# A fused attention and MLP-mixer kernel: the order, PSUM banks and gates of every queue read from a table instead of a list scheduler, and one fp32r matmul woven with two bf16 ones

## The chip, the cores and the metric

The kernel runs on one core of one Trainium2 chip. The metric is the device time of one execution, in microseconds (us); lower is better. Before the change three runs took 354.62, 355.6 and 358.28 us, so the median is 355.6 us.

## The reference

Eight batches of a linear attention with eight heads, then a mixer block on its output; everything is given and returned in fp32.

```python
kv  = einsum('bhsd,bhse->bhde', k, v)            # B=8, H=8, S=576, D=64
out = einsum('bhsd,bhde->bhse', q, kv)
out = out / sqrt(mean(out*out, -1) + 1e-6) * g_norm
x   = out.transpose(0,2,1,3).reshape(8, 576, 512)
a1  = alpha1*x + beta1
u   = x + lam * einsum('ts,bsd->btd', w_tok, a1)     # token mixing, 576 x 576
a2  = alpha2*u + beta2
y   = u + lam * (relu(a2 @ w_ch1) @ w_ch2)           # channel mixing, 512 -> 2048 -> 512
```

## The kernel before

The program is written in two steps. First the body of the kernel records operations ("ops") with what they read and write; each op gets an index in the order in which it is recorded (0 to 1415), and belongs to one queue: PE (TensorE), ACT, DVE, POOL or SP. A PE op holds several matmuls (`mm`, line 120); the others hold one instruction or one DMA. `_add` (line 75) derives the dependencies. Then `schedule` (line 135) orders everything, `synchronize` (line 387) works out the semaphore waits that this order needs, and `emit` (line 447) writes the instructions. Each engine executes its queue strictly in the order that comes out.

`schedule` is a list scheduler. It plays the program on a clock of its own: every op has a cost guessed from its size, due times are propagated backwards from the main stream of matmuls, a table `P.shift` (line 1283) moves single ops, and a table `P.gate` (line 1298) adds dependencies ("op 9 after op 31"). PE has two streams. The main one (`ch1`, `ch1_tail`, `ch2`) goes in its recorded order; the fill stream (all else) is put between where it is ready, with a margin of 0.3 us. PSUM has eight banks of 128x512 fp32; main ops take banks 0 to 3 in turn, fill ops banks 4 to 7.

Where a ready fill op of fp32r matmuls meets a ready main op of bf16 matmuls, the two become one unit and are woven (line 428): one fp32r matmul, one bf16 matmul, and so on. While the main stream has not begun, an fp32r or fp32 op is woven with throw-away matmuls on the tile `fil` instead (`idler`, line 379; L597 in the profile), which keep TensorE busy.

What the work is, by the names that the prediction uses:

- Start. SP loads q, k and v of batch 0 in pairs of heads (`load_pair`, L611, 288 KB each), four pairs of q of batch 1, and the token weights (`wl`, L629, 1152 KB; `wlt`, L631, 144 KB). `qt_early` (L698 on POOL, L703 on PE) transposes q, `kv_first` (L725) makes k'v, `norm_half` (L864) multiplies by q and normalises (L807 to L833). `wt_group` (L1081, L1084) transposes the token weights; ACT copies them to bf16 (L1087); `wsums` (L1103, L1110, L1113, L1118) adds rows of sums. `tok_half` (L929) is the token mixing of batch 0, its result is added to x on DVE (L937), `a2_pair` (L968, L972) transposes that into the layout for the channel mixing.
- Steady state, for each batch: `kv` (L749, L755, then L766 on ACT and L768 on DVE) and `norm` (L843, then Square on ACT L807, DVE L810, ACT L813, DVE L816 to L825), all fp32r matmuls of 128 columns; `tok` (L914, bf16, five matmuls of 512 columns, added on DVE L921); `a2_dma` (two POOL instructions, L986 and L989, and a transposing DMA from SP, L993); `ch1` (L1002, four matmuls of 512 columns, relu on ACT L997) sixteen times, `ch2` (L1031, four units of four matmuls for each of four blocks of tokens), `finish` (DVE L1058, POOL or DVE L1063, a store from SP, L1066). The last 64 tokens of two batches go together (`tok_tail` L948, `ch1_tail` L1014).
- Weights of the channel mixing come in five transfers issued by POOL (`load_w1` L1163, `load_w2` L1169) between its other work, in the same POOL queue as the loads of k and v (`load_kv`, L1186, L1190).
- End. The last block of tokens of the last batch is cut into 256, 128 and 128 columns (L1042), each with its own `finish` and two small stores (L1070).

The weave before is these lines:

```python
    def woven(f, m):                      # line 428: f fp32r, m bf16
        out, i, j = [], 0, 0
        n, k = len(f.fns), len(m.fns)
        while i < n or j < k:
            if i < n and (j >= k or i * k <= j * n):
                out.append((f, i)); i += 1
            else:
                out.append((m, j)); j += 1
```

Of the kernel before, what the change touches and what calls it, by code (L numbers as in the profile page):

```python
# [11 lines left out]
ACT = mybir.ActivationFunctionType  # L12
# [11 lines left out]

class Op:


    __slots__ = ("bias", "q", "kind", "cost", "lat", "fns", "pri", "idx", "deps", "raw", "alloc",
                 "tiles", "start", "end", "pos", "waits", "inc", "clock", "slot", "nbytes",
                 "val", "margin", "tag", "narrow", "urgent", "ns")  # L30

    def __init__(self, q, kind, cost, lat, fns, pri, idx):
        self.q, self.kind, self.cost, self.lat = q, kind, cost, lat
        self.fns, self.pri, self.idx = fns, pri, idx
        self.deps, self.raw = set(), set()
        self.alloc, self.tiles = [], []
        self.start = self.end = self.pos = None
        self.waits, self.inc, self.clock = [], False, None
        self.slot = self.nbytes = self.val = self.ns = None
        self.margin = 0.0  # L40
        self.tag, self.narrow, self.urgent = "", False, False
# [12 lines left out]
class Prog:  # L54
    ENGINES = ("PE", "ACT", "DVE", "POOL")

    def __init__(self, nc, stack):
# [7 lines left out]
        self.main, self.fill = [], []  # L65
        self.bias = 0.0
        self.reach = 24
        self.warm, self.began, self.early, self.lead = 6.0, False, 45.0, 100.0
        self.t0, self.pace, self.last, self.shift = 31.0, 1.28, None, {}
        self.gate = {}  # L70
# [4 lines left out]
    def _add(self, o, r, w, after):  # L75
# [10 lines left out]
        for key in w:  # L86
# [21 lines left out]
    def op(self, q, cost, fn, r=(), w=(), pri=0.0, lat=0.15, after=()):  # L108
        o = Op(q, "c", cost, lat, [fn], self.bias + pri, len(self.ops))
        o.bias = self.bias  # L110
        return self._add(o, r, w, after)

    def dma(self, q, slot, nbytes, fn, r=(), w=(), pri=0.0, after=(), issue=0.55):
        o = Op(q, "d", issue, 0.0, [fn], self.bias + pri, len(self.ops))
        o.slot = slot
        o.nbytes, o.ns = nbytes if isinstance(nbytes, tuple) else (nbytes, 20.0)
        o.bias = self.bias
        return self._add(o, r, w, after)

    def mm(self, stream, cols, fns, r=(), w=(), slow=False, after=(), margin=0.3,  # L120
           urgent=False):

        n = len(fns)
        per = cols * MM_NS + 0.0025
        each = slow if isinstance(slow, float) else {"r": 0.213}.get(slow, 0.109)
        o = Op("PE", "w" if slow and each is not slow else "m",
               n * (max(per, each) if slow else max(per, 0.056)),
               0.24, fns, self.bias, len(self.ops))
        o.bias = self.bias
        o.margin, o.narrow, o.urgent = 0.0 if urgent else margin, cols < 512, urgent  # L130
        (self.main if stream == "main" else self.fill).append(o)
        return self._add(o, r, w, after)


    def schedule(self):
        for i, j in self.gate.items():
            self.ops[i].deps.add(self.ops[j])
        due, t = {}, self.t0
        for o in self.main:
            due[o] = t  # L140
            t += o.cost * self.pace
        after = {}
        for o in self.ops:
            for y in o.deps:
                after.setdefault(y, []).append(o)
        order, left = [], {o: len(after.get(o, ())) for o in self.ops}
        stack = [o for o in self.ops if not left[o]]
        while stack:
            o = stack.pop()
            order.append(o)  # L150
            for y in o.deps:
                left[y] -= 1
                if not left[y]:
                    stack.append(y)
        for o in order:
            d = due.get(o, 1e6)
            for y in after.get(o, ()):
                if y in due:
                    d = min(d, due[y] - o.cost - o.lat - (2.5 if o.kind == "d" else 0.0))
            if d < 1e6:  # L160
                due[o] = d
        for o in self.ops:
            if o.kind == "d":
                o.pri += self.shift.get(o.idx, 0.0)
            elif o in due and o.pri - o.bias > -900:
                o.pri = due[o] + self.shift.get(o.idx, 0.0)
            elif o.pri - o.bias > -900:
                o.pri = 1e4 + o.pri
        self.fill.sort(key=lambda o: o.pri)
        queues = {e: [] for e in ("ACT", "DVE", "POOL", "SP")}  # L170
        for o in self.ops:
            if o.q != "PE":
                queues[o.q].append(o)
        for q in queues.values():
            q.sort(key=lambda o: (o.pri, o.idx))
        main, fill = list(self.main), list(self.fill)
        self.main0 = set(self.main)
        free = {e: 0.7 for e in list(queues) + ["PE"]}
        owner = [None] * 8
        rings = {e: deque() for e in ("SP", "POOL", "ACT")}  # L180
        t, left = 0.0, len(self.ops)
        events = {0.7}
        self.sequence = []
        self.idle = []
        last_fill = False
        INF = 1e9

        def ready_at(o):
            m = 0.0
            for y in o.deps:  # L190
                if y.end is None:
                    return INF
                m = max(m, y.end - y.lat if y.q == o.q == "PE" else y.end)
            return m

        def bank_at(b):
            x = owner[b]
            if x is None:
                return -1.0
            m = 0.0  # L200
            for y in x.ops:
                if y.end is None:
                    return INF
                m = max(m, y.end)
            return m

        def place(o, t):
            got = []
            for tile in o.alloc:
                c = [(bank_at(b), b) for b in self.pools[tile.pool] if b not in got]  # L210
                c = [x for x in c if x[0] <= t + 1e-9]
                if not c:
                    return None
                got.append(min(c)[1])
            return got

        def can(o, t, margin=0.0):
            return ready_at(o) + margin <= t + 1e-9 and place(o, t) is not None

        def take(o, t, cost=None):  # L220
            nonlocal left
            for tile, b in zip(o.alloc, place(o, t)):
                tile.bank = b
                if owner[b] is not None:
                    o.deps.update(owner[b].ops)
                owner[b] = tile
            o.start = t
            if o.kind == "d":
                rings[o.q].append([o, t + (1.9 if o.q == "POOL" else 1.1), o.nbytes, False, o.ns,
                                   o.slot[0] == "t"])  # L230
            else:
                o.end = t + (o.cost if cost is None else cost) + o.lat
                events.add(o.end)
            if o.margin:
                events.add(o.end + 0.3)
            left -= 1

        def begin(a):
            for r in rings.values():
                if r and r[0][1] <= a + 1e-9:  # L240
                    r[0][3] = True

        def heads():
            return [r[0] for r in rings.values() if r and r[0][3]]

        def soonest(h):
            whole = sum(x[4] for x in h)
            return min(x[2] * whole / x[4] for x in h)

        def flow(a, z):  # L250

            while True:
                if not heads():
                    begin(a)
                h = heads()
                n = min([a + soonest(h) if h else min([r[0][1] for r in rings.values() if r] + [z]),
                         z])
                whole = sum(x[4] for x in h)
                for x in h:
                    x[2] -= (n - a) * x[4] / whole  # L260
                done = [x for x in h if x[2] <= 1e-6]
                for r in rings.values():
                    if r and r[0][3] and r[0][2] <= 1e-6:
                        r.popleft()
                a = n
                if done:
                    begin(a)
                for x in done:
                    o = x[0]
                    if x[5]:  # L270
                        rings[o.q].appendleft([o, a + 0.6, 0.05, False, 20.0, False])
                    else:
                        o.end = a + (0.1 if o.slot[0] == "t" else 2.0 if len(h) > 1 else 1.2)
# [1060 lines left out]
```

## Time and profile before

| What | Value |
|---|---|
| Runs | 354.62, 355.6, 358.28 us (median 355.6) |
| Profiled execution, span from its first to its last instruction | 354.8 us |
| Instructions | 5512 |
| TensorE matmul busy | 341.3 us (96%), 2208 matmuls |
| VectorE (DVE) busy | 189.8 us (54%) |
| ScalarE (ACT) busy | 149.0 us (42%) |
| GpSimd (POOL) busy | 161.4 us (45%) |
| Moved by DMA | 48.76 MB, mean 137 GB/s |

The profiled execution's own time is its span, 354.8 us; it lies 0.8 us under the median of the runs shown. A line of the profile names the source line, engine and operation, then what is written and read ("ps<-w,hh" writes PSUM from two tiles). Matmuls are pipelined: the record of one lasts longer than the time until the next can start, so a matmul's price is read from the distance of starts. PEclk is the granted TensorE clock, 1 or 9 being full speed.

### The profile page before, as it was taken

The numbers are of one execution on the slowest core, as the hardware profiler recorded it, in microseconds if no ns is written. First come the engines' busy times: TensorE is split into PE (matmuls) and PEld (weight loads), VectorE is DVE, ScalarE is ACT, GpSimd is POOL, SyncE is SP. The second block draws the span as 40 slices with busy tenths as digits, with TensorE's granted clock in tenths as the row PEclk, the third lists the DMA queues.
The fourth block names the chain that finished last, engine by engine and source line by source line (L and its number), as shares of the span: only waits on it lengthen the run. The fifth ranks groups of instructions, "written<-read, shape, count | busy, mean of one in ns | idle before, by whom it ended". The sixth has DMA issues, their size and how long they took to land.

```text
span 354.8 us, 5512 instructions
## 1 busy us (share of the span) xinstructions
PE 341.3 (96%) x2208; PEld 198.4 (56%) x2241; DVE 189.8 (54%) x343; ACT 149.0 (42%) x291; POOL 161.4 (45%) x151
## 2 busy tenths in 40 slices
PE   4979999999999999999999999999999999999994
PEld 3858964454664664466556545564476444444644
DVE  3475778204685579636745676459444963210043
ACT  3335397004940386126823366136552273026400
POOL 2397410965308940985058612973192306930000
PEclk9989999999999999999999999999999999999999
DMA  7999899969598399138963995239922110330012
GB/s 241 267 336 161 139 251 230 144 110 198 120 262 134 90 232 213 31 93 195 247 61 76 221 173 124 46 116 258 175 33 89 59 31 15 75 105 0 2 69 79
DMA packets 107952, 48.76 MB, mean 137 GB/s; under 512 B 81997, under 2 KB 99925, under 8 KB 107928
## 3 DMA queue, kind: packets, MB, share of 16 engines
q1 hardware_dynamic: 82312, 27.71, 42.9%
q0 software_dynamic: 25616, 20.71, 34.0%
q8 instruction: 17, 0.28, 0.3%
q14 instruction: 7, 0.06, 0.1%
HBM read 38.82 MB, written 9.44 MB: 136 GB/s over the span
## 4 chain that ended last, share of the span: by engine, by line
PE 87%; DMA 5%; SPq 2%; POOL 2%; DVE 1%; issue 1%; ACT 0%; DVEq 0%; POOLq 0%
PE ps L1031 31%; PE ps L1002 31%; PE ps L914 8%; PE ps L1014 4%; PE ps L843 3%; DMA hh<-in_moe_w_tok_dram 2%; PE ps L749 2%; DMA w<-in_k_dram 2%; PE ps L597 1%; SPq L611 1%; PE ps L929 1%; POOL a1f L986 1%; PE ps L948 1%; PE ps L1081 1%; PE ps L1042 1%; DMA lam_bc<-in_moe_lam_dram 1%
## 5 line engine op out<-in xcount | busy, mean ns | idle before, releaser
L1031 PE MATMUL ps<-w,hh 128*128 128x512 bf16 x543 | 135.3, 383 | 0.7 <-issue 0.3
L1002 PE MATMUL ps<-a2m,w 128*128 128x512 bf16 x501 | 117.8, 381 | 1.0 <-DVE tmp L1058 0.4
L997 ACT ACTIVATE hh<-ps 128x512 bf16<-128x512 f32 x144 | 84.8, 597 | 64.3 <-PE ps L1002 54.9
L1031 PEld LDWEIGHTS ps<-w,hh 128*128 128x128 bf16 x560 | 52.9, 97 | 58.8 <-issue 1.6
L1002 PEld LDWEIGHTS ps<-a2m,w 128*128 128x128 bf16 x512 | 48.7, 98 | 56.5 <-DVE tmp L1058 1.3
L986 POOL TENSOR_TENSOR a1f<-xm,a_bc 128x512 f32<-128x512 f32 x28 | 35.5, 1273 | 68.6 <-DVE xm L921 68.3
L1058 DVE TENSOR_TENSOR tmp<-ps,lam_bc 128x512 f32<-128x512 f32 (+2 forms) x38 | 25.1, 661 | 69.8 <-PE ps L1031 56.5
L1063 POOL TENSOR_TENSOR xm<-xm,tmp 128x512 f32<-128x512 f32 x28 | 35.4, 1269 | 34.7 <-DVE tmp L1058 34.7
L810 DVE TENSOR_REDUCE small<-sq 128x8 f32<-128x512 f32 (+2 forms) x41 | 27.2, 666 | 25.2 <-ACT sq L807 25.0
L989 POOL TENSOR_TENSOR a2b<-a1f,b_bc 128x512 bf16<-128x512 f32 x32 | 40.3, 1273 | 0.7
L843 PE MATMUL ps<-kvc,qt 128*128 128x128 f32 x140 | 40.1, 395 | 0.0
L921 DVE TENSOR_TENSOR xm<-ps,xm 128x512 f32<-128x512 f32 x28 | 19.3, 690 | 29.8 <-PE ps L914 28.5
L749 PE MATMUL ps<-vr,kr 128*128 128x128 f32 x112 | 32.3, 395 | 0.0
L807 ACT ACTIVATE sq<-ps 128x512 f32<-128x512 f32 (+2 forms) x41 | 23.9, 584 | 19.3 <-PE ps L843 18.5
L1199 ACT ACTIVATE qt<-qp 128x576 fp32r<-128x576 f32 x24 | 15.9, 682 | 32.3 <-DVE qp L1196 32.3
L843 PEld LDWEIGHTS ps<-kvc,qt 128*128 128x128 f32 x140 | 27.4, 199 | 2.0
L914 PE MATMUL ps<-rm,wt 128*128 128x512 bf16 x109 | 28.3, 379 | 0.2
L597 PE MATMUL ps<-fil 128*128 128x128 bf16 x109 | 20.0, 245 | 4.5 <-DVE fil L596 4.5
L819 DVE TENSOR_TENSOR ps<-ps,small 128x512 f32<-128x512 f32 (+1 forms) x35 | 23.5, 690 | 0.5
L766 ACT ACTIVATE kvo<-ps 64x256 f32<-64x256 f32 x14 | 5.3, 378 | 43.0 <-PE ps L755 42.8
L749 PEld LDWEIGHTS ps<-vr,kr 128*128 128x128 f32 x112 | 22.3, 201 | 0.9
L1196 DVE STREAM_TRANSPOSE qp<-qs 128x576 f32<-128x576 f32 x24 | 17.3, 755 | 5.6 <-DMA qs<-in_q_dram 3.4
(109 smaller groups left out, 324.0 us busy)
## 6 DMA issues: line engine op xcount, KB each, us to landing
out_dram<-xm SPq DMA_DIRECT2D x32, 256.0 KB, 2.3
kr<-in_k_dram POOLq DMA_DIRECT2D x7, 1024.0 KB, 9.0
vr<-in_v_dram POOLq DMA_DIRECT2D x7, 1024.0 KB, 11.4
qs<-in_q_dram SPq DMA_DIRECT2D x24, 288.0 KB, 11.1
w<-in_moe_w_ch_dram POOLq DMA_DIRECT2D x3, 1024.0 KB, 10.2
xm<-in_q_dram SPq DMA_DIRECT2D x8, 288.0 KB, 4.4
w<-in_k_dram SPq DMA_DIRECT2D x4, 288.0 KB, 5.6
qs<-in_v_dram SPq DMA_DIRECT2D x4, 288.0 KB, 5.9
```

The source lines that it names most:

```text
L749: P.mm("fill", 128, [lambda e, t=t, c=c, h=h, o=128 * (h % 4): e.matmul(t.ap()[:, o:o + 128], kr4[:, h, c:c + 2, :].rearrange("p c d -> p ...
L807: P.op("ACT", act(n), lambda e: e.activation(sq[rs, s3, 0:nst, :].rearrange("p h e -> p (h e)"), ps(), ACT.Square), r=[t], w=[("sq", s3)])
L810: P.op("DVE", dve(n), lambda e: e.tensor_reduce(out=st, in_=sq[rs, s3, 0:nst, :], axis=AX.X, op=ALU.add), r=[("sq", s3)], w=[("sm", s4)])
L843: P.mm("fill", 128, [lambda e, p=p: e.matmul(dst(p), qt[:, p, cs], kvc[:, i, p, :], start=(p == 0), stop=(p == 3)) for p in range(4)], r=[ ...
L914: P.mm("fill", 512, [lambda e, sc=sc: e.matmul(t.ap(), wt[:, sc if sc < 4 else tw(b), 128 * c:128 * c + 128], rsrc(b, sc, al), start=(sc = ...
L986: P.op("POOL", pool(512), lambda e: e.tensor_tensor(out=a1f[:, s], in0=x, in1=a2_bc[:], op=ALU.mult), r=ks + ["a2"], w=[("a1f", s)])
L989: P.op("POOL", pool(512), lambda e: e.tensor_tensor(out=a2b[:, c], in0=a1f[:, s], in1=b2_bc[:], op=ALU.add), r=[("a1f", s), "b2"], w=[("a2 ...
L997: P.op("ACT", act(512), lambda e: e.activation(dst, t.ap(), ACT.Relu), r=[t], w=keys, pri=-1000)
L1002: P.mm("main", 512, [lambda e, dj=dj: e.matmul(t.ap(), w1[:, dj, 128 * fj:128 * fj + 128], a2m[:, b % 3, dj, :], start=(dj == 0), stop=(dj ...
L1031: P.mm("main", 512, [lambda e, fj=fj, t=t, c=c: e.matmul(t.ap(), (ht[:, fj, 128 * c:128 * c + 128] if c < 4 else hl[:, fj, :]), w2[:, fj, ...
L1058: P.op("DVE", dve(z - a), lambda e: e.tensor_tensor(out=tmp[:, s, a:z], in0=t.ap()[:, 0:z - a], in1=lam_bc[:, a:z], op=ALU.mult), r=[t, "l ...
L1063: lambda e: e.tensor_tensor(out=x, in0=x, in1=tmp[:, s, a:z], op=ALU.add),
```

## The change

The functions that build ops are unchanged, and so are the ops and their indices. What is replaced is everything that decides order. `schedule` with its costs, due times, margins and DMA model is gone, and so are `P.shift`, `P.pace` and the two PE streams. In its place stands a table `ORDER` of 1302 units, and `replay`, which walks it. A number is an op; `:1` behind it gives the PSUM bank of the tile that the op opens (any bank for any op); `+` joins ops into one woven PE unit; `~28` is a block of 28 throw-away matmuls. `GATES`, a new table of 54 added dependencies, takes the place of `P.gate`, which had 26.

```diff
+ORDER = """
+31 5 1 25 23 6 0 26 12 ~28 27 9 10 15 40 8 7 24 41 14 3 19 4 16 42:1 46:2 44:3 109 18 ~20 17 45
...
+351:6+273:3+330 270 267 274 271 214 352+334+332 180 216 275 272 333 276 343 280 331 277 339 281
...
+1395 1400:0 1396 1377 1401 1409 1397 1410 1402 1390 1398 1411 1403 1399 1412 1413 1391 1404 1405
+1415 1406 1407 1414
+"""
+GATES = {11: 16, 13: 3, 17: 0, 18: 15, 19: 12, 21: 26, 24: 26, 37: 75, 39: 41, 105: 73, 106: 227,
...
-    def schedule(self):
...
+    def replay(self, order, gates):
+        for i, j in gates.items():
             self.ops[i].deps.add(self.ops[j])
...
+        for word in order.split():
+            if word[0] == "~":
+                self.sequence.append((self.idler(int(word[1:])),))
+                continue
+            unit = []
+            for part in word.split("+"):
+                at, *banks = part.split(":")
+                o = self.ops[int(at)]
+                for tile, b in zip(o.alloc, banks):
+                    tile.bank = int(b)
+                    if owner[tile.bank] is not None:
+                        o.deps.update(owner[tile.bank].ops)
+                    owner[tile.bank] = tile
+                unit.append(o)
+            self.sequence.append(tuple(unit))
...
-    def woven(f, m):
+    def woven(f, *ms):
+        a = [(f, i) for i in range(len(f.fns))]
+        b = [(m, j) for m in ms for j in range(len(m.fns))]
         out, i, j = [], 0, 0
-        n, k = len(f.fns), len(m.fns)
+        n, k = len(a), len(b)
...
-                    if not isinstance(key, Bank) and key[0] == "sm":
+                    if not isinstance(key, Bank) and key[0] in ("sm", "tmp"):
...
-        P.schedule()
+        P.replay(ORDER, GATES)
```

The PE queue holds the same matmuls. Before, 99 units weave two ops; after, 13 weave two and 55 weave three (one fp32r op of four matmuls with two bf16 ops of four or five). In the steady state the 256 fp32r matmuls mostly stood as fp32r, bf16, fp32r, bf16; after, 208 of them have two bf16 matmuls on either side. The throw-away matmuls were 109, 72 of them woven with fp32r and fp32 matmuls of the start; after, they are 113 in nine blocks of their own (28, 20, 21, 6, 8, 7, 8, 12, 3), woven with nothing.

Other moves that the prediction speaks of: the loads of k and v of batch 1 (L1186) now stand behind more of POOL's work at the start, the first of them behind the ACT copy of the token weights' last rows (op 97); the six `norm_half` units of the start all stand ahead of the `wt_group` transposes (before, two stood behind them); the order of `ch1` and `ch2` units in a batch is free, with banks 0 to 7 for both; at the end, the store of the last full block (op 1391) stands behind the two stores of the 256-column piece, and four more small stores behind that. ACT has a second table load, since a copy (L716) now stands ahead of the first square root.

More of the change, by code (lines that the diff above doesn't have):

```diff
@@ L132, in mm @@
+        o.form = (stream, cols, slow)
         return self._add(o, r, w, after)
[L135 to L136 removed]
+    def replay(self, order, gates):
+        for i, j in gates.items():
             self.ops[i].deps.add(self.ops[j])
[L138 to L178, printed above, removed]
```

259 lines of the change are left out of this document (31 added, 228 removed), and 83 rows, old and new, of tables (GATES, ORDER, cs).

## The prediction

> **What bounds the kernel now.** I read the page first, then busy time by stage, then the order of time inside the stages.
>
> ```profile
> span 354.8 us, 5512 instructions
> PE 341.3 (96%) x2208; PEld 198.4 (56%) x2241; DVE 189.8 (54%) x343; ACT 149.0 (42%) x291; POOL 161.4 (45%) x151
> PEclk9989999999999999999999999999999999999999
> PE 87%; DMA 5%; SPq 2%; POOL 2%; DVE 1%; issue 1%; ACT 0%; DVEq 0%; POOLq 0%
> ```
>
> ```profile
> 0.00:23.90 23.90, 16.89 (x224) 13.72 (x224) 11.59 (x31) 9.52 (x24) 10.22 (x19) 1.00 0.90 271
> 23.90:44.37 20.47, 20.31 (x197) 18.01 (x199) 13.17 (x25) 7.42 (x16) 12.67 (x13) 0.92 1.15 179
> 44.37:350.32 305.95, 304.15 (x1788) 166.72 (x1818) 164.47 (x286) 132.04 (x252) 138.52 (x120) 1.00 0.75 125
> 350.32:354.80 4.48, 0.00 (x0) 0.00 (x0) 0.58 (x2) 0.00 (x0) 0.00 (x0) 1.00 0.23 59
> ```
>
> The second fence is busy time by stage (window, its length, then PE, PEld, DVE, ACT, POOL, clock, DMA share, GB/s). Four stages: loads until the token weights land (23.9 us), from there to the first channel matmul (20.5), the steady state (306.0, of which PE is busy 304.2), and the end (4.5). PE is 87% of the chain that ended last; in the steady state only fewer PE nanoseconds can help, while the second stage is worth looking at, since much of PE's work in it is thrown away.
>
> **The weave.** First its price before, from the timeline of a woven stretch, of one at the start with matmuls of 256 columns, and from the chain, for bare matmuls of 128 columns.
>
> ```profile
> 121.16 0.39 PE L1031 MATMUL ps<-w,hh 128*128 128x512 bf16 x1
> 121.20 0.41 PE L755 MATMUL ps<-vr,kr 128*128 128x128 f32 x1
> 121.45 0.39 PE L1031 MATMUL ps<-w,hh 128*128 128x512 bf16 x1
> 122.03 2.12 PE L1031 MATMUL ps<-w,hh 128*128 128x512 bf16 x9
> ...
> 37.55 0.31 PE L749 MATMUL ps<-vr,kr 128*128 128x128 f32 x1
> 37.70 0.39 PE L929 MATMUL ps<-rm,wt 128*128 128x256 bf16 x2
> 37.85 0.30 PE L749 MATMUL ps<-vr,kr 128*128 128x128 f32 x1
> 37.99 0.28 PE L929 MATMUL ps<-rm,wt 128*128 128x256 bf16 x1
> 38.03 0.31 PE L749 MATMUL ps<-vr,kr 128*128 128x128 f32 x1
> ```
>
> ```profile
> 97.13 3.57 PE ps L1014 x64
> ```
>
> Nine bare bf16 matmuls of 512 columns take (2.12 - 0.39)/8 = 0.216 us each; a woven pair takes 121.45 - 121.16 = 0.29. So an fp32r matmul adds 0.075. Does it add less behind two bf16 ones? The second stretch has both forms: from one fp32r to the next 0.30 with two matmuls between, 0.18 with one. The second costs 0.12 more, and a bare one of that size costs 0.109 by my reading of starts (an estimate: half of 0.216). Nothing is saved, so I take 0.075 for all 256, and the weave at 0. Ends: 0.056 (the bare 128-column matmul, 3.57/64) if the rest is hidden by the second cover, 256 x 0.019 = 4.9 us less, and 0.08 above, 1.3 us more.
>
> The Trainium skill, "TensorE: Matmul & The Clock Gate", section "Back-to-back issue gap", gives N/2.4 + 2.5 ns per matmul, 56 ns at 128 columns, and "Step-by-step: what each phase is for" lets the next weights load while the present matmul runs; by that rule a longer cover could bring the fp32r matmul to 56 ns. The rows at 37 us speak against it.
>
> The steady-state program is the same set of matmuls: 1212 of 512 columns x 0.216 = 261.8, 256 fp32r x 0.075 = 19.2, 256 of L1014 x 0.056 = 14.3, and 9.2 for the tails (40 L948, 48 L1042) and eight transposes: 304.5. The window has 305.95, so PE stalls only 1.4 us in all.
>
> **The start.** PE from the landing of the token weights, from the chain in order of time:
>
> ```profile
> 15.58 8.33 DMA hh<-in_moe_w_tok_dram
> ...
> 24.37 0.21 PE ps L1081
> 24.69 0.21 PE ps L1081
> ...
> 29.62 0.12 PE ps L1081
> 29.79 0.12 PE ps L1081
> ```
>
> *Landing.* The weights land at 23.9. What SP sends ahead of them stays the same (twelve pairs of 288 KB, three of batch 1, 144 KB), with them 5.75 MB; the first window moved 271 GB/s x 23.9 = 6.5 MB, the rest being the loads of batch 1 on POOL's queue. Those now issue some 4 us later. At 271 GB/s alone 5.75 MB is there at 21.2; I take 22.8, between that and 23.9. The new gates on SP make SP wait for landings, but its queue holds four or five loads at each such wait, so nothing runs dry: cost 0; if it does, each empty us comes on top.
>
> *PE's lane.* A transpose with its thrown-away partner steps 0.32 us cold, 0.17 warm; by itself 0.21 or 0.12. The clock of this window is 0.92, after 2 us without work. The change puts only 7 + 8 fillers (0.9 us) ahead of the weights, so I assume cold again: 16 transposes at 0.21, four plus four at 0.12, the sixth group done 4.4 us after landing. Warm would save 1.1 us. The Trainium skill, same page, section "What's actually happening", has the clock go full after about 3.4 us of work and back after an idle window as long; the cold stretch here, 24.0 to 27.4, agrees, though 2 us of idleness were enough.
>
> *DVE's lane* is next, since PE's fillers are gone from it. DVE's queue from there to the last sum that the first `a2_pair` units need holds the same 17 instructions as this window, but for one:
>
> ```profile
> 30.20:40.60 10.40, 8.66 (x17) 1.00 0.61 94
> ...
> L831 DVE TENSOR_TENSOR rm<-xm,e_bc 128x512 bf16<-128x512 f32 x2 | 1.9, 944 | 0.0
> ```
>
> 8.66 us, plus the slower L831 (2 x 0.944 less 0.68, so 1.21) for one copy of 0.69: 9.2. Starting 4.4 + 0.2 after landing, it ends at 13.8. Behind it PE has four woven fp32r with four transposes (0.75), `tok_half` (0.55), transposes (0.44), and ACT the copy L972 (0.78), with 0.3 for hand-overs: 2.8. I add 0.4 for waits inside the lane. First channel matmul at 22.8 + 13.8 + 2.8 + 0.4 = 39.8 instead of 44.4: **4.6 us earlier.** Ends: 38.2 (landing 21.6, warm for half) and 42.5 (landing 23.9, waits 2 us).
>
> *The weights behind it.* POOL issues the second quarter of w1 after a product (L833) that needs DVE's lane at 12 us, so at 36.3 instead of 37.1. The next one landed 37.9 + 10.2 = 48.1, 11.0 after that:
>
> ```profile
> 37.12 1.55 POOL L1163 DMA_DIRECT2D w<-in_moe_w_ch_dram  x2 [3.40 <-ACT small L813]
> ...
> w<-in_moe_w_ch_dram POOLq DMA_DIRECT2D x3, 1024.0 KB, 10.2
> ```
>
> It lands at 47.3 then. The new order uses it 8.1 us of PE work after the first channel matmul, at 47.9. The old order used it 9.9 us of PE work after the first channel matmul, at 54.3, some 6 us later than it landed; now 0.6 are left. So a start earlier than 39.2 gains nothing: that is the floor.
>
> *ACT's second table load* (1.28 us) runs before the copies of `kv_first`:
>
> ```profile
> 0.73 1.28 ACT L599 ACT_TABLE_LOAD   x1 [0.73 <-PEq L1319]
> 12.24 0.45 ACT L739 ACTIVATE kvc<-ps 64x64 fp32r<-64x64 f32 x2 [3.06 <-PE ps L725]
> ```
>
> ACT waits 3.06 us for PE there, so it costs 0; without that cover 1.3. The added wait for `tmp` (DVE for its own older add) is met long before: 0.
>
> **The steady state.** Before, the banks of the main stream went round in fours, so PE came back to a bank three units (2.6 us) after filling it. In the new order PE comes back to the relu of the unit before last 15 times, after one unit of four matmuls, 0.864 us, and 21 times within 1.2 us. The round trip, from the timeline and the chain:
>
> ```profile
> 50.93 0.81 PE L1002 MATMUL ps<-a2m,w 128*128 128x512 bf16 x3
> 51.11 1.26 ACT L997 ACTIVATE hh<-ps 128x512 bf16<-128x512 f32 x2
> ```
>
> ```profile
> 49.30 0.49 ACT hh L997
> 49.84 1.90 PE ps L1002 x8
> ```
>
> PE's last matmul streams until 51.36 + 0.22; ACT's second relu begins at 51.11 + 1.26 - 0.60 = 51.77, 0.19 later; it takes 0.60, and PE goes on 0.05 after a relu (49.79, 49.84). That is 0.84 of 0.864: it fits only if ACT is free, and between relus ACT also squares (0.60) and takes roots (0.30). Behind a waiting unit the whole PE queue waits. I take 0.1 for each of 21, so 2.1 us; ends 0 (the table knew it) and 0.45 (half of the ACT instructions' time that may lie ahead, three times in four), 9 us. Of the 1.4 before, 0.5 goes: lam was late,
>
> ```profile
> 77.35 3.54 DMA lam_bc<-in_moe_lam_dram
> 80.98 0.70 DVE tmp L1058
> ```
>
> ```profile
> L989 POOL TENSOR_TENSOR a2b<-a1f,b_bc 128x512 bf16<-128x512 f32 x32 | 40.3, 1273 | 0.7
> ...
> a2m<-a2b SPq DMA_TRANSPOSE x28, 2.5
> ```
>
> and now its load stands right behind one load of q, some 8 us earlier. Next late are the transposes of batch 1: the first `tok` to be used ends about 61.4, its add 62.3, then eight POOL instructions of 1.27 and an issue (0.7) to 73.2, and 2.5 for the transpose, 75.7; PE uses it 35.6 us of work after 39.8, with half a us of stalls at 75.9. So I keep nothing for it, and keep 0.3 of the rest, since consecutive fp32r matmuls are gone. 304.5 + 0.3 + 2.1 = 306.9, **0.9 more.**
>
> **The end.**
>
> ```profile
> 349.48 3.68 SPq L1071 DMA_DIRECT2D out_dram<-xt  x6
> 350.68 0.29 DVE L1063 TENSOR_TENSOR xt<-xt,tmp 128x128 f32<-128x128 f32 x1
> ...
> out_dram<-xt SPq DMA_DIRECT2D x4, 32.0 KB, 1.9
> ```
>
> SP issues one store per 0.61 us here, and the last, 2.2 after PE's end, lands 1.9 later. In the new order DVE adds the last full block after the 256-column piece; its store issues 0.25 after PE's end with four small ones behind it, the last at about 3.2. **0.9 more.** Ends: 0 and 1.5.
>
> **The sum**, against the profiled execution: 354.8 - 4.6 + 0.9 + 0.9 = 352.0. The median of the runs is 0.8 above that span: 352.8.
>
> **The rivals.**
> A, the fp32r matmul is hidden by two covers: all else as above, 4.9 us less, 347.9. For it speak the weight load of 0.2 us; against it the rows at 37 us.
> B, the table is a good clock: start at the floor (39.2), no stalls above the old ones less lam (305.4), end unchanged (4.5): 349.1, with 0.8 349.9. For it: the order has waits at 0.864 where I measure 0.84, so it knew the round trip.
> C, slower than before: ACT late at the tight round trips. It decides from 0.1 + 2.8/21 = 0.23 us per round trip; at 0.35 the stalls are 7.4 and the time 358.1. For it: PE now depends on ACT within one unit; against it: 42% busy ACT, and an order fitted to durations.
> D, the start gains nothing, because the weights land as before and DVE's lane waits (first channel matmul at 43): 356.0.
>
> **How the numbers follow.** The forecast, 352.8 with its own range of 351 to 354.5, has a chance of 0.40 (a fifth of it below 352.0); A 0.10, B 0.23, C 0.15, D 0.12. A measurement of this kernel tells about 1%, 3.6 us. Faster by that: A, B and 0.08 of the forecast, 0.41. Slower by that, above 359.2: the part of C with 0.4 us and more per round trip, 0.06. Within it: 0.53. The range of 349.0 to 357.0 leaves out A, the upper part of C and the lowest part of B.
>
> **What would show it.** Right: first L1002 near 40 us; a triple (fp32r, bf16, bf16) taking 0.507; idle time of PE before L1002 put down to ACT L997 of about 2 us in all; last store issued 3 us after PE's last matmul. Wrong: triples of 0.49 or less; L1002 waiting for POOL's weights around 48 us; no idle time with ACT; a start at 43.

## The result, and the profile after

| | before | after |
|---|---|---|
| Time, median of 4 runs | 355.15 us (354.62 to 358.28) | 376.69 us (374.46 to 377.64) |
| Ratio | 1 | 1.0589, 95% interval 1.0529 to 1.0649 |
| Profiled execution, span | 354.8 us | 375.0 us |
| Start to the first channel matmul | 44.4 | 43.2 |
| From there to the end of PE's last matmul | 305.95 | 325.95 |
| PE's end to the last landing | 4.5 | 5.8 |

The change made the kernel 21.5 us slower; 352.8 was predicted, 349 to 357 the range. Nearly all of it lies in the steady state, the stage for which 0.9 us more was forecast: the two profiled executions are 20.2 us apart, and this stage 20.0, while the start is 1.2 shorter and the end 1.4 longer. The page after, with the chain's shares in its last line:

```profile
span 375.0 us, 5537 instructions
...
PE 345.7 (92%) x2210; PEld 199.2 (53%) x2245; DVE 187.1 (50%) x343; ACT 144.7 (39%) x292; POOL 161.5 (43%) x151
...
PEclk9969999998999999999999859999999999999999
...
PE 66%; DMA 10%; DVE 8%; SPq 5%; POOL 5%; ACT 2%; issue 2%; DVEq 0%; POOLq 0%
```

Busy time by stage (window, length, PE, PEld, DVE, ACT, POOL, clock, DMA share, GB/s):

```profile
0.00:23.07 23.07, 17.96 (x267) 15.22 (x268) 9.03 (x28) 9.83 (x23) 6.52 (x15) 0.99 0.80 264
23.07:43.18 20.11, 19.06 (x159) 17.06 (x161) 13.65 (x28) 8.40 (x20) 15.73 (x17) 0.85 1.01 162
43.18:369.13 325.95, 308.67 (x1786) 166.88 (x1818) 163.26 (x284) 126.47 (x252) 139.20 (x121) 0.98 0.68 119
369.13:374.96 5.83, 0.00 (x0) 0.00 (x0) 1.12 (x5) 0.00 (x0) 0.00 (x0) 0.92 0.31 94
```

PE was busy 304.2 of 306.0 us in this stage before; now 308.7 of 326.0. The work is the same, so 17.3 us are idle, and of the 4.5 us of extra busy time some 4 are matmuls at half clock, as shown below: PEclk has two dips in this stage that the page before does not have. PE's waits (in total, times, longest):

```profile
PE ps L847 <- DMA a2m<-a2b: 12.7, 2, 9.7
...
PE ps L759 <- DVE xm L670: 1.5, 1, 1.5
...
PE ps L594 <- ACT hh L842: 0.7, 1, 0.7
```

Two waits for a transposing DMA (L838, the last step of `a2_dma`) make up 12.7 us; waiting for ACT's relus, the forecast's only new stall, is 0.7. The larger one, in PE's timeline:

```profile
209.22 0.41 PE L688 MATMUL ps<-kvc,qt 128*128 128x128 f32 x1
219.37 0.58 PE L847 MATMUL ps<-a2m,w 128*128 128x512 bf16 x1 [9.74 <-DMA a2m<-a2b]
...
220.29 4.96 PE L847 MATMUL ps<-a2m,w 128*128 128x512 bf16 x14
```

PE stands still for 9.7 us, and then fourteen matmuls take (4.96 - 0.39)/13 = 0.35 us each instead of 0.216. SP's queue at that time, after and then before, tells why the transpose was late:

```profile
195.38 1.22 SPq L838 DMA_TRANSPOSE a2m<-a2b  x1
197.90 0.32 SPq L1023 DMA_DIRECT2D qs<-in_q_dram  x1
198.27 4.46 SPq L838 DMA_TRANSPOSE a2m<-a2b  x2
202.77 10.76 SPq L1023 DMA_DIRECT2D qs<-in_q_dram  x2
213.57 3.86 SPq L838 DMA_TRANSPOSE a2m<-a2b  x1
```

```profile
183.95 6.34 SPq L993 DMA_TRANSPOSE a2m<-a2b  x3
...
192.79 1.20 SPq L993 DMA_TRANSPOSE a2m<-a2b  x1
...
195.25 17.65 SPq L1178 DMA_DIRECT2D qs<-in_q_dram  x4
```

Before, the four transposes of batch 4 go first (the last lands at 195.2, and PE first uses them at 203.6), and the four loads of q for the next batch behind them, where they hold SP for 17.65 us and harm nobody. In the table three loads stand between the transposes. Two of them hold SP for 10.8 us, and the fourth transpose is issued at 213.6. The two are far from equal, as the shortest, median and longest of the two issues show (in ns):

```profile
L1023 SPq DMA_DIRECT2D qs<-in_q_dram x2: 630/5356/10082, 202.8 to 203.4; - x2
```

So a price per load, here and below, is a mean: of the four loads before, the shortest took 0.3 us and the longest 9.2. The loads of q are not the whole of it either: the two transposes issued ahead of them, at 198.3 and 200.5, landed only at 209.5 and 212.1, with POOL's loads of k and v issued from 198.3 on. The smaller stall has the same look in batch 1 (PE, then SP):

```profile
83.56 1.59 PE L847 MATMUL ps<-a2m,w 128*128 128x512 bf16 x4 [2.94 <-DMA a2m<-a2b]
```

```profile
70.40 3.16 SPq L838 DMA_TRANSPOSE a2m<-a2b  x2
73.69 1.05 SPq L1023 DMA_DIRECT2D qs<-in_q_dram  x1
74.78 1.41 SPq L1068 DMA_DIRECT2D lam_bc<-in_moe_lam_dram  x1
76.23 0.43 SPq L1023 DMA_DIRECT2D qs<-in_q_dram  x1
76.71 5.49 SPq L838 DMA_TRANSPOSE a2m<-a2b  x2
```

Theory Q: the new order puts loads of q ahead of transposes in SP's strict queue, as if a load cost SP its 0.7 us (the `issue` argument at L1023), when one of them took 10.1. The rivals: the weave (W), PE's bank order and ACT (R, B), DMA engines that are full in any order (D), POOL's chain of products (P), the gates (G).

### The profile page after: what moved, and what is told of

Same layout as the page of the kernel before. It is cut to its first block, busy times and chain, and to the rows that moved or that the text cites. A ratio compares the mean times of both kernels' runs of the same rounds, so it can differ in the third digit from the quotient of the medians.

```text
span 375.0 us, 5537 instructions
## 1 busy us (share of the span) xinstructions
PE 345.7 (92%) x2210; PEld 199.2 (53%) x2245; DVE 187.1 (50%) x343; ACT 144.7 (39%) x292; POOL 161.5 (43%) x151
## 4 chain that ended last, share of the span: by engine, by line
PE 66%; DMA 10%; DVE 8%; SPq 5%; POOL 5%; ACT 2%; issue 2%; DVEq 0%; POOLq 0%
PE ps L876 24%; PE ps L847 22%; PE ps L759 7%; DMA w<-in_moe_w_ch_dram 4%; PE ps L859 4%; SPq L1023 3%; DMA a2m<-a2b 3%; DMA a_bc<-in_moe_alpha_dram 2%; POOL a1f L831 2%; POOL a2b L834 2%; PE ps L688 2%; ACT hh L842 2%; DMA w<-in_k_dram 2%; SPq L838 1%; PE ps L594 1%
## 5 line engine op out<-in xcount | busy, mean ns | idle before, releaser
L847 PE MATMUL ps<-a2m,w 128*128 128x512 bf16 x499 | 124.6, 389 | 13.9 <-DMA a2m<-a2b 12.7
L842 ACT ACTIVATE hh<-ps 128x512 bf16<-128x512 f32 x144 | 80.6, 597 | 102.8 <-PE ps L847 98.1
L847 PEld LDWEIGHTS ps<-a2m,w 128*128 128x128 bf16 x512 | 44.5, 100 | 63.1 <-issue 13.2
L876 PEld LDWEIGHTS ps<-w,hh 128*128 128x128 bf16 x560 | 43.8, 98 | 44.5 <-issue 0.8
L688 PE MATMUL ps<-kvc,qt 128*128 128x128 f32 x140 | 52.6, 402 | 0.1
L594 PE MATMUL ps<-vr,kr 128*128 128x128 f32 x112 | 41.5, 389 | 0.7 <-ACT hh L842 0.7
L594 PEld LDWEIGHTS ps<-vr,kr 128*128 128x128 f32 x112 | 21.0, 191 | 11.5 <-ACT hh L842 0.8
L664 DVE TENSOR_TENSOR ps<-ps,small 128x512 f32<-128x512 f32 (+1 forms) x35 | 24.2, 696 | 0.7
L859 PEld LDWEIGHTS ps<-a2l,w 128*128 128x128 bf16 x256 | 16.5, 98 | 5.9
L668 DVE TENSOR_TENSOR rm<-ps,e_bc 128x512 bf16<-128x512 f32 x28 | 18.8, 678 | 0.2
```

What stands on the lines that cost most here:

```text
L594: P.mm("fill", 128, [lambda e, t=t, c=c, h=h, o=128 * (h % 4): e.matmul(t.ap()[:, o:o + 128], kr4[:, h, c:c + 2, :].rearrange("p c d -> p ...
L688: P.mm("fill", 128, [lambda e, p=p: e.matmul(dst(p), qt[:, p, cs], kvc[:, i, p, :], start=(p == 0), stop=(p == 3)) for p in range(4)], r=[ ...
L842: P.op("ACT", act(512), lambda e: e.activation(dst, t.ap(), ACT.Relu), r=[t], w=keys, pri=-1000)
L847: P.mm("main", 512, [lambda e, dj=dj: e.matmul(t.ap(), w1[:, dj, 128 * fj:128 * fj + 128], a2m[:, b % 3, dj, :], start=(dj == 0), stop=(dj ...
L859: P.mm("main", 128, [lambda e, dj=dj, fj=fj: e.matmul(t.ap()[:, 128 * fj:128 * fj + 128], w1[:, dj, 128 * (f4 + fj):128 * (f4 + fj) + 128] ...
L876: P.mm("main", 512, [lambda e, fj=fj, t=t, c=c: e.matmul(t.ap(), (ht[:, fj, 128 * c:128 * c + 128] if c < 4 else hl[:, fj, :]), w2[:, fj, ...
```

## The experiments

Each is one kernel. Where the edit is in the table, the diff shows the words of one queue only, in their order. Times are medians; ratios are to the kernel before on the same chip, with 95% intervals. "The loss" is against the kernel before.

**1. Loads of q behind the transposes, batch 4.**

```diff
 SP
-758 869 748 743 870 868 753 508
+758 748 743 753 869 870 868 508
```

> One edit of the table on the changed kernel: in batch 4 the three loads of q that stand on SP's queue between the transposes (ops 869, 870, 868) move behind the fourth transpose (753). Theory Q (the time was lost in the order of SP's queue): each such load holds SP for about 4.4 to 5.4 us, so the last transpose lands some 10 us earlier, the 9.9 us without work at 209 us go, and with them the about 2.9 us of matmuls at half clock behind it: 376.7 - 12.8, about 364. Rival D (the transposes are late because loads on all queues share the DMA engines): transposes issued ahead still land late, at most 3 us gained, 374 or more. Rival R (the lost time belongs to PE's bank order and its round trips through ACT): the stall goes and another takes its place within the batch, 372 or more.

Measured: 367.5 us (364.99 to 370.21), ratio 1.034 (1.026 to 1.043), 9.2 less than the change. The largest single part of the loss is shown to be SP's order in batch 4. But 3.6 of the 12.8 us did not come:

```profile
210.53 0.38 PE L847 MATMUL ps<-a2m,w 128*128 128x512 bf16 x1 [2.58 <-DVE tmp L903]
...
211.02 6.18 PE L847 MATMUL ps<-a2m,w 128*128 128x512 bf16 x20
```

A stall of 2.6 us had been hidden inside that of 9.7: a product on DVE, and a transpose landing at 210.4, almost as late.

**2. Pairs instead of triples.** The diff is one unit of 54.

```diff
-352+334+332
+352+334 332
```

> The changed kernel with its 54 woven triples (one fp32r matmul to two bf16 ones) split: the first two units woven one to one, the third behind them, bare. Theory Q has the weave at nothing (0.075 us per fp32r matmul under either cover): 376.7 within 1. Rival W (the second bf16 matmul hides part of the fp32r matmul, up to 0.019 us in each of 216): up to 4.1 us slower, 381. Opposite rival (the triples cost time that the pairs did not): faster by 2 us or more.

Measured: 376.96 us (375.18 to 379.35), ratio 1.061 (1.053 to 1.069) against 1.059 for the change. No worth of the weave shows either way, within an interval of 0.8%. Rival W at its most (4.1 us) would make a triple 0.49 us; it takes 0.51, as shown further down, so W is out.

**3. The second half of w2 later.**

```diff
 POOL
-178 210 212 179 211 265 260
+178 210 212 211 265 179 260
```

> One edit of the table on the changed kernel: the load of the second half of w2 (op 179, 1 MB) moves on POOL's queue from 45.4 us to behind the first product of the a2 chain (op 265), about 62 us, so that it is no longer under way when the a and b rows are loaded. Theory Q: those rows land some 3.5 us earlier (about 61.5 instead of 65.1), POOL's a2 chain and the four transposes of batch 1 follow, the 3.1 us without work at 80.3 us go and the 1.8 us at half clock behind them: 372. Rival: POOL's chain is late for another reason (its own length of 13.5 us from 66.5, with the load of vrt inside it), the rows land as late as before: 376 to 377; or w2 is now late for the channel matmuls: 377 or more.

Measured: 381.4 us (380.66 to 382.41), ratio 1.072 (1.064 to 1.080). Theory Q misses, and both halves of its rival hold. The a row landed at 65.2, as before (65.1), so this load was not what delayed it; and PE's list of waits has a new row, since the table uses this half of w2 early:

```profile
PE ps L876 <- DMA w<-in_moe_w_ch_dram: 4.3, 1, 4.3
```

**4 and 8. The start.** The transposes of the token weights go ahead of what stood before them on PE.

```diff
 PE, run 4
-54 ~8 56 196 ~7 82 88 94 91 85 198 ~8
+54 56 82 88 94 91 85 196 ~8 ~7 198 ~8
 PE, run 8
+54 56 82 88 94 91 85 196 198
```

> One edit of the table on the changed kernel: on PE's queue the transposes of the token weights (ops 82, 88, 94, 91, 85) move ahead of the 15 fillers and of the four transposes of q that stood before them, right behind the second row of e1. Theory P (PE's own queue gave away the earlier landing of the weights): the transposes begin at 23.7 instead of 26.4, DVE's lane follows, first channel matmul at about 40.5 instead of 43.0; the end follows by what the next stalls leave of it, since the load of w1 and the a and b rows land no earlier: 375 to 376.5, and the stall at 61.6 or 80 us longer. Rival L (DVE's or POOL's lane sets the first channel matmul, not PE): it stays at 42.5 to 43.

> The start again, without what spoiled the last try (there the fillers were moved behind the transposes of the weights, ahead of the transposes of q that DVE waits for): the three groups of fillers (23 matmuls) between e1 and the sums are left out, and the transposes of q stand behind those of the weights. They are thrown-away matmuls, so the output is untouched. Theory P: DVE's lane begins at about 29.1 instead of 30.5 and the first channel matmul at 41.7 instead of 43.2; at 80 us the a2 chain takes it back, time within 1 of the changed kernel. Rival C (the fillers keep the clock up, and the lane is as late without them): first channel matmul at 43 or later.

Measured: 377.3 us (376.08 to 378.64), first channel matmul at 44.2; and, for the second try, 374.3 (373.75 to 374.8, two runs), first channel matmul at 45.5. Theory P is not borne out: PE's transposes began at 24.2 and 25.0 instead of 26.2, and the first channel matmul came no earlier (43.2 in the change). In run 4 DVE's lane began at 31.2 instead of 30.5, since the transposes of q that it waits for now stood behind those of the weights. DVE's products, in run 4 and in run 8, and POOL's in run 8 show where the second try lost time:

```profile
32.78 1.29 DVE L676 TENSOR_TENSOR rm<-xm,e_bc 128x512 bf16<-128x512 f32 x1
...
34.82 0.42 DVE L676 TENSOR_TENSOR rtl<-xt,e_bc 64x256 bf16<-64x256 f32 x1
```

```profile
33.83 1.34 DVE L676 TENSOR_TENSOR rtl<-xt,e_bc 64x256 bf16<-64x256 f32 x1
```

```profile
33.64 1.25 POOL L678 TENSOR_TENSOR xm<-xm,g_bc 128x512 f32<-128x512 f32 x1
```

The same 64x256 product takes 0.42 us in one and 1.34 in the other, where POOL runs a product of its own until 34.9. Moved earlier, DVE's lane runs into POOL's. The Trainium skill, "SBUF — State Buffer", section "SBUF: two separate sides", has DVE and GpSimd share a pair of ports under an exclusive lock, the loser waiting for the other's whole instruction; the rows agree with that, DVE's product ending 0.3 us after POOL's. Then PE waited for DVE and went on slowly:

```profile
35.87 1.04 PE L774 MATMUL ps<-rm,wt 128*128 128x256 bf16 x4 [2.40 <-DVE wt L958]
```

The same four matmuls take 0.61 us in the change; the clock was 0.50 from 35.3 to 38.7 us. So the first channel matmul came late, as rival C had it; but that the missing fillers are the reason is not shown, since run 6, which keeps them, fell to half clock there too (from 34.9 on, after 1.7 us without work).

**5 and 6. Batch 1, what stands behind w2 on SP.**

```diff
 SP, run 5
-106 182 105 181
+106 105 182 181
 L1069, run 6, besides
-                after=[P.lastw[("w2", 0)][0]])
+                after=[P.lastw[("w2", 0)][0]] if key == "lam" else [])
```

> One edit of the table on the changed kernel: on SP's queue the second copy of the token weights (op 105) moves ahead of the load of the b row (op 182), which waits at the queue's head for w2 until 56.5 us. Theory Q: the token matmuls at 63.5 us waited for this copy, which landed at 63.1, not for the sum on DVE that the profile names: the copy lands at about 50, the 1.5 us without work go, and the stall at 80 us grows by as much, since the a2 chain is where it was: time within 1 of the changed kernel. Rival V (DVE's norm sums set it, as the profile names): the stall at 63.5 stays at 1 us and more.

> The edit of the run before, and in the code the loads of the a and b rows no longer wait for w2 to land; they stand right behind the two copies of the token weights on SP's queue, at about 44 us. Theory Q (both stalls of batch 1 are SP's queue standing behind w2): the rows land by 52, POOL's a2 chain begins with DVE's sum at about 62.5 instead of 66.5 and the last transpose lands at 79.5 instead of 83.5, when PE, 1.5 us earlier, wants it at 79: of 1.5, 3.1 and the 1.8 us of matmuls at half clock some 5.5 go, 371. Rival D (the DMA engines are full there, whatever the order): the rows or w1 land later, the transposes with them, 375 or more. Rival P (POOL's chain is what is long): the stall of 3 us stays, 374.

Measured: 375.8 us (two runs, 374.88 to 376.62) and 377.3 (375.83 to 377.69). In run 5 the stall that ended at 63.5 fell from 1.5 to 0.6 us and that at 80 grew to 3.4, so the copy of the weights did set it, and the time is unchanged, as forecast. Run 6 is a miss: the b and a rows landed at 54.0 and 55.5, some nine us earlier, but the last transpose, counted from the first channel matmul, only 0.6 earlier, and the stall stayed (3.2 us). POOL shows what its chain waited for:

```profile
67.23 2.50 POOL L831 TENSOR_TENSOR a1f<-xm,a_bc 128x512 f32<-128x512 f32 x2 [9.76 <-DVE xm L766]
```

It waited for DVE's second sum (66.5 to 67.1), not for the rows.

**7. Batch 4 in full.**

```diff
 SP as in run 1; POOL
-751 864 865 866 672 752 816 823 837
+751 672 752 816 823 864 865 866 837
 DVE
-900 901 886 903 836 878
+900 836 901 886 903 878
 gates
+864: 753
```

> The edit of the first run (loads of q behind the fourth transpose of batch 4) and two more in the same place: POOL's loads of k and v for the next batch (864 to 866) go behind the four products and wait for the fourth transpose (753) to land, and the product with lam (836) moves on DVE's queue ahead of three steps of a norm. Theory Q: what was left at 210 us in the first run, 2.6 us without work and about 1.6 at half clock, was half a transpose slowed by the loads of k and v (landed 210.4) and half DVE's order (done 210.3); with both mended 3 to 4 us go against the first run: 363.5. Rival: PE's bank order leaves another stall within 10 us of it, no gain against the first run (367.5).

Measured: 366.4 us (366.07 to 367.62), ratio 1.032 (1.025 to 1.038). No wait of PE at 210 is left. Against run 1 that is 1.1 us, not 3 to 4, and the intervals overlap; the two spans differ by 0.7. SP's queue prices the loads of q anew:

```profile
196.88 6.12 SPq L838 DMA_TRANSPOSE a2m<-a2b  x4
203.12 4.36 SPq L1023 DMA_DIRECT2D qs<-in_q_dram  x3
```

1.5 us each in the mean, with POOL's loads of k and v issued from 206.6 on. In run 1, with the loads of q in the same place but POOL's issued from 196.6 on and still under way, it was 2.9 (8.8 for three); 5.4 in the change, where POOL's were issued from 198.3 on; 4.4 in the kernel before, from 195.7 on.

**9. The cost put into the kernel before.**

```diff
 P.schedule()
+at = {o.idx: u for u in P.sequence for o in u}
+P.sequence.remove(at[753])
+P.sequence.insert(P.sequence.index(at[871]) + 1, at[753])
```

> The suspected cost added to the kernel before: in batch 4 its third transpose on SP's queue (op 753, ready in time) moves behind the four loads of q (868 to 871) that it stood ahead of. Nothing else changes, weave and bank order are those of before. Theory Q: the fourth load ends its issue at about 212 us, the transpose lands at 214 to 217, PE wants it at about 203.5: 10 to 13 us without work and some 3 at half clock, 355.4 + 13 to 16, about 370. Rival (the changed bank order and weave are needed for the loss): within 2 of the kernel before.

Measured: 369.8 us (368.19 to 371.62), ratio 1.039 (1.032 to 1.047): one transpose behind four loads of q (the change has three among its transposes) costs the unchanged kernel 14 us. SP and PE:

```profile
194.47 17.24 SPq L1178 DMA_DIRECT2D qs<-in_q_dram  x4
211.75 2.31 SPq L993 DMA_TRANSPOSE a2m<-a2b  x1
```

```profile
215.84 4.42 PE L1002 MATMUL ps<-a2m,w 128*128 128x512 bf16 x10 [12.92 <-issue]
```

The profile names no releaser ("issue"); the transpose landed at 215.7. Together with run 1 this settles the main cause: taken away it gives back 9 us, added it costs 14.

**10 and 11. Batch 1's loads of q alone, and all queues together.**

```diff
 SP, run 10
-262 267 214 180 216 272 277 215 217
+262 267 180 272 277 214 216 215 217
 run 11: runs 5, 7 and 10 in one
```

> One edit of the table on the changed kernel: in batch 1 the loads of q (214, 216) move behind the fourth transpose (277) on SP's queue. Its product is done at 77.5 us, and it was issued at 80.9, since the two loads and the transpose queued behind them held SP. Theory Q: transposes issued by 78 and landed by 81, PE wants them at 80.5: the stall of 2.9 us falls to 0.5 or less and the clock stays: 372.5. Rival P (POOL's chain): stall of 2 us and more, 375.5.

> All mends of the queues together on the changed kernel: batch 4 as in the run that moved loads of q, k and v and a product with lam; and in batch 1 the two loads of q (214, 216) behind the fourth transpose (277) on SP's queue, and the copy of the token weights (105) ahead of the b row. Theory Q: against that run (366.4) the stall of 3.4 us at 81 us goes with the 2.2 us at half clock, and 0.6 at 63: 360 to 361, of which the rest above the kernel before is small stalls (about 3 us), the end (1.4) and less 0.7 at the start. Rival P (POOL's chain of products, not SP, is late in batch 1): 365.5.

Measured: 374.8 us (two runs, 374.03 to 375.61), ratio 1.053 (1.044 to 1.063), and 362.35 (362.11 to 365.08), ratio 1.021 (1.013 to 1.029). In both the stall at 80 us is gone, so it too was the loads of q ahead of the transposes, and rival P is out. SP in run 11 issues the last two transposes without them (3.28 us for two, where the change has 5.49 from 76.7 on):

```profile
73.42 3.28 SPq L838 DMA_TRANSPOSE a2m<-a2b  x2
```

But neither time came as forecast. Run 10 is not told apart from the change (1.059), and the steady state of run 11 is only 2.6 us shorter than that of run 7 (312.8 against 315.3), for a new stall ends at 89; its PE and DVE:

```profile
89.36 1.04 PE L847 MATMUL ps<-a2m,w 128*128 128x512 bf16 x4 [2.16 <-ACT hh L842]
```

```profile
87.33 2.31 DVE L1041 STREAM_TRANSPOSE qp<-qs 128x576 f32<-128x576 f32 x3 [4.68 <-DMA qs<-in_q_dram]
```

The name ACT is misleading: ACT's relu stood behind copies that waited for DVE's transposes of q, and these for the loads, landed at 87.3. Now q is late.

**12. No gates.** The table `GATES` is empty.

> The changed kernel without its gates: the second table empty, so that loads wait only for their data and buffers; orders and banks as changed. Theory Q (orders, not gates, cost the time): within 3 of the changed kernel, 374 to 380, since loads set free earlier stand ahead of the transposes in the DMA engines a little more. Rival G (the gates' waits at the head of SP's queue are what holds the transposes): faster by 5 us or more.

Measured: 383.05 us (two runs), ratio 1.076 (1.067 to 1.086), 6 slower than the change and above the 374 to 380 expected. Rival G is out: taken together, the gates help. Both stalls for transposes stay (12.2 us), and one of 4.1 for DVE at 270 us is new.

**13 and 14. Loads of q early, and the end.**

```diff
 SP, run 13 (from run 11; gate 214: 269 goes)
-182 181 262 267 180 272 277 214 216 215 217
+182 181 214 215 216 262 267 180 272 277 217
 in the call of load_q
-P.lastw[("w2", 2)][0]
+P.lastw[("w2", 0)][0]
 run 14, besides: DVE, then SP
-1376 1396 1397 1390 1412
+1376 1390 1396 1397 1412
-1377 1398 1399 1391 1415
+1377 1391 1398 1399 1415
```

> The kernel with all queues mended, once more. There the loads of q of batch 1, moved behind its transposes, landed at 87.3 us, and DVE and ACT, in order, waited for q ahead of two relus: 2.8 us without work at 89 us and 1.3 at half clock. Now three of the four loads go ahead of the transposes, into the time when SP was empty (57 to 69 us): in the code they wait for the first half of w2 instead of the second, and one gate goes. Theory Q (what is left is still the price of q's loads on SP): the stalls at 87 to 93 us go, 4 us, and time is 358 to 359. Rival D (DMA engines full): the a and b rows, the second half of w2 or the transposes land later and stalls of 2 us and more come back at 75 to 82 us, 362. Rival B (bank order through ACT): the stall at 89 us stays, 362.

> The run before it and one more edit: at the end DVE's sum of the last full block (op 1390) goes ahead of the two steps of the 256-column piece, and its store (1391) ahead of that piece's two. Theory E (after PE the stores queue on SP one per 0.6 us behind a store that came late): the last store issues about 1 us earlier, 1 us less than the run before. Rival: the queue of small stores behind the last DVE step sets the end, no change.

Measured: 363.4 us (360.5 to 365.67), ratio 1.020 (1.012 to 1.027), and 363.07 (362.77 to 364.2), ratio 1.019 (1.015 to 1.023). The stall at 89 went and that at 81 came back, as rival D had it. Run 14's waits and SP's last stores:

```profile
PE ps L847 <- DMA a2m<-a2b: 2.1, 1, 2.1
...
PE ps L594 <- ACT hh L842: 0.9, 1, 0.9
PE ps L847 <- DMA w<-in_moe_w_ch_dram: 0.7, 1, 0.7
```

```profile
354.77 0.94 SPq L911 DMA_DIRECT2D out_dram<-xm  x2
356.16 4.56 SPq L916 DMA_DIRECT2D out_dram<-xt  x6
```

The end is as long as it was (PE's last matmul ends at 356.3, 6.1 before the span's end): the microsecond that theory E promised is not there (run 13 has 6.4, and the kernels with the end of the change lie between 5.3 and 6.4), and the queue of small stores sets the end. The table interleaves the last two pieces on PE, so both are ready only when PE is done, and SP still has their four stores to issue, 0.6 us each.

No mended version beats the kernel before, so none was carried further. Of its 20.0 us of loss in the steady state, run 14 has 6.3 left (312.3 against 306.0): the rows above and small ones of 0.2 to 0.7, from many queues. Which order would remove them stays open.

## Why the prediction was wrong

*The steady state, 0.9 more; measured 20.0 more.* The step that failed is the one that summed it as PE work, a few round trips and 0.3: "in the steady state only fewer PE nanoseconds can help". True of the old order, it was carried to a new one without asking what else the new one moved. SP's queue was read for the start, where gates were called free because it "holds four or five loads at each such wait", and for batch 1; for batches 2 to 7 no queue but PE's was compared. The diff of SP's order has the three loads of q between the transposes, and the old profile had their price in one row (17.65 us for four). Three loads at that price are 13 us of SP time ahead of a transpose that had 8 us to spare (195.2 to 203.6). That this order costs the time is shown by runs 1 and 9; the 6.3 us that run 14 keeps are not explained.

*Batch 1's transposes.* The forecast has them land at 75.7 for use at 75.9: "So I keep nothing for it". Two tenths of slack at the end of a chain of ten steps is a coin's toss. The forecast had the first product at 62.3; it began at 66.5, but 3.4 of these 4.2 us are the late first channel matmul, which moves the use as well. Counted from there, the fourth product was done 1.6 us later than forecast (77.5), and what the forecast left out comes next: on SP two loads of q and lam stand between the products and the transposes. The fourth transpose was issued 3.5 us after its product, at 80.9, landed at 83.5, and PE had run out of work at 80.6: 2.9 us idle, and some 1.7 lost at half clock. That the loads on SP decide is shown by run 10.

*lam, 0.5 gained.* Forecast 8 us earlier; it landed at 80.4 instead of 80.9, behind the same loads. What that could have gained lies under the stall of 2.9 us.

*The round trips through ACT, 2.1 us.* PE waited 0.7 us for ACT after the start. Rival C had the sign right, but not the cause: transposes late on SP, not relus late on ACT.

*The weave, 0.* Right. From a triple in the change:

```profile
122.29 0.60 PE L876 MATMUL ps<-w,hh 128*128 128x512 bf16 x2
122.54 0.41 PE L600 MATMUL ps<-vr,kr 128*128 128x128 f32 x1
122.80 2.55 PE L876 MATMUL ps<-w,hh 128*128 128x512 bf16 x10
```

From 122.29 to 122.80 is 0.51 for two bf16 and one fp32r matmul, 0.43 + 0.075, and run 2 finds no difference.

*The start, 4.6 earlier; measured 1.2.* The landing was right (23.07 for 22.8). The lane behind it was not: PE's queue had e1's second row, 15 fillers and four transposes of q ahead of the weights.

```profile
22.97 1.03 PE L442 MATMUL ps<-fil 128*128 128x128 bf16 x8
...
24.55 1.11 PE L548 MATMUL ps<-ident,qp 128*128 128x128 f32 x4
25.45 0.95 PE L442 MATMUL ps<-fil 128*128 128x128 bf16 x7
26.20 3.86 PE L926 MATMUL ps<-ident,hh 128*128 128x128 f32 x20
```

The forecast let the transposes start at the landing; they start 3.1 later. That PE's delay is all of the missing 3.4 us is not shown: runs 4 and 8 removed part of it and gained nothing. The first channel matmul lay between 41.5 and 44.8 in the eleven kernels that keep this start, and the clock has a part in that: run 11, with 41.5, had a clock of 1.00 from 20 us on, and the change 0.50 from 24 to 28 us. Rival D's start at 43 came (43.2), but not because the weights landed as before.

*The end, 0.9 more; measured 1.4.* The mechanism, small stores behind the last DVE steps, was right. That the store of the last full block is the cause is not borne out: issued ahead of the small ones in run 14, it left the end at 6.1.

## What to carry to other kernels

When an order changes, compare every in-order queue, not only that of the busiest engine: for each transfer on which the main stream waits, list what now stands ahead of it and price that by the old profile's rows, as a range where the price moves with other queues (1.5 to 5.4 us per load of q here). A price that the old order hid (17.65 us of SP behind the transposes) is still a price, and a table fitted with a wrong one moves work into it. Where a stall is mended, look for the next one inside it; here each mend gave back between none and three quarters of what its stall, with the half clock behind it, had cost.

## What the runs showed of the hardware

- Issuing one load of q on SP took 1.5 us in the mean of three in run 7, and 2.9 in run 1, where loads of k and v from POOL's queue were under way; 4.4 and 5.4 in the kernels before and after. Single issues lay between 0.3 and 10.1. The price of an instruction in a queue depends on what another queue is moving.
- Idle time of PE can cost twice. After 2.9 and 9.7 us without work in the change the next matmuls ran at half clock (0.427 from start to start instead of 0.216), some 1.7 and 2.2 us in all; after 2.6 us at 208 in run 1 too. But the length of the gap alone does not decide: after 3.2 us at 80 in the same run 1 the clock stayed full, as it did after 3.2 in run 6 and 2.1 in run 14:

```profile
83.69 1.04 PE L847 MATMUL ps<-a2m,w 128*128 128x512 bf16 x4 [3.22 <-DMA a2m<-a2b]
```

  That is run 1, (1.04 - 0.39)/3 = 0.217 each. The Trainium skill, "TensorE: Matmul & The Clock Gate", section "What's actually happening", has the clock fall back after an idle window of about 3.4 us; here 2.6 were enough once, and two gaps of 3.2 were not.
- The releaser that the profile names can be a bystander: DVE's L670 at 63.5 us stood for a copy of weights (run 5), and ACT's relu at 89 us for loads of q two engines away (run 11).
